# Attention with beacon keys and a max-out layer: values steps and second-layer tiles at other places of a written step list

## Chip, cores and metric

The kernel runs on one core of one Trainium2 chip. The metric is device time in microseconds from the start to the end of one execution; the figure of a kernel is the median over its runs. The profile is of one further execution, whose own time stands beside it.

## What is computed

```python
k_all = np.concatenate([beacon_k, k], axis=2)          # B, H, S, D = 8, 8, 576, 64; 16 beacons
v_all = np.concatenate([beacon_v, v], axis=2)
scores = scale * np.matmul(q, k_all.transpose(0, 1, 3, 2))
scores = np.where(causal, -1e9, scores)                # beacons are seen by every query
a = softmax(scores)
x = np.matmul(a, v_all)  -> (B * S, H * D) = (4608, 512)
h = np.maximum(np.maximum(x @ w1, x @ w2), x @ w3)     # 512 -> 768, three times
out = h @ w_out                                        # 768 -> 512, float32
```

## The kernel before

The whole program is one list of steps, `first_steps + loop_steps`, written out by hand. `emit_all` walks it from top to bottom and calls one helper for each step, so the order of the list is the order of the instructions on each of the engines; a step that issues on several engines takes its place in the order of each. No planner moves anything later. Engines wait for one another by semaphores only where a step reads what another has written, or where it reuses a tile.

The attention works on pairs of heads (32 pairs, four to a batch) and on quads, two pairs each (16 quads, two to a batch: quads 2b and 2b + 1 are of batch b). The steps that matter:

- `("scores", p, g, 0, place)` computes one of four groups of key tiles and queries for pair p: 2 or 4 matmuls (L513) into a PSUM tile, then one exponential on ScalarE (L522) into SBUF. `("mask", p, g, "pool")` zeroes the causal part there on POOL (L541). The groups of a pair come in the order 0, 2, 3, 1.
- `("values", quad, half, place)` is the softmax's sums and the product with v for one half of the queries of a quad, 120 matmuls for both halves (L582; 44 and 76). The first half needs groups 0, 2 and 3 of both pairs, the second needs all.
- `("invert",)` takes the reciprocal of the sums on ScalarE by a logarithm and an exponential (L603, L605); `("multiply", 3)` are three products on VectorE (L615) that write the quad's part of x; `("cross x", k, g, e, "pool")` copies it to the other half of the partitions on POOL (L680), which the first layer needs.
- `("unit", place)` is a piece of the first layer: 16 matmuls (L699) for 128 of the 768 outputs of one of the three weights and a block of tokens (two halves of 288), then a maximum (or, for the first weight, a copy) on VectorE into hT (L631, L629). There are 18 units to a block; the units of the block of batch b are dealt between the scores steps of batch b + 1, so that TensorE has work while ScalarE and POOL finish the scores.
- `("out", n, place)` is the second layer for n tiles of 128 tokens: 6 matmuls of 512 columns per tile (L725), a copy on VectorE (L733); `("store", 1)` sends the result by a DMA from the SP queue (L759).
- `("load", n)` issues the next input DMAs from the SP queue, behind a small memset on VectorE or POOL where an engine is named; `cast`, `cross`, `pair`, `keys` and `cast v` bring inputs into the form that scores and values need.

`place` is one of four PSUM tiles, 0 to 3. A step that takes a place waits until the step that had it before has been read out. Most places in the list are reused four uses later; some after two or three.

In a batch the list deals scores steps and units in turn. The values steps of the batch before come at two points: the even quad's ("first values steps") after unit 9 of the block, just behind the first two scores steps of the batch's third pair, and the odd quad's at the end of the block, behind unit 17. Quad 4 has its values step one unit earlier than the other even quads. An out of two tiles stands ahead of most first values steps and one of one to three tiles behind the last ones.

At the start, while the first inputs arrive, `("busy", n, cols)` issues n matmuls on a constant tile (L477).

Of the kernel before, what the change touches and what calls it, by code (L numbers as in the profile page):

```python
# [16 lines left out]
def kernel(  # L17
# [119 lines left out]
    busy = const.tile([128, 320], BF16, name="busy")  # L137
# [698 lines left out]
    def start_late():  # L836
# [62 lines left out]
        ("busy", 31, 174),  # L899
        ("identity",),  # L900
        ("busy", 12, 213),
# [230 lines left out]
        ("values", 4, 0, 2),  # L1132
        ("invert",),
        ("values", 4, 1, 3),
# [12 lines left out]
        ("mask", 10, 3, "pool"),  # L1147
        ("unit", 3),
        ("scores", 10, 1, 0, 0),
        ("mask", 10, 1, "pool"),  # L1150
        ("unit", 1),
        ("scores", 11, 0, 0, 2),
        ("mask", 11, 0, "pool"),
        ("unit", 3),
        ("load", 1, "pool"),
        ("scores", 11, 2, 0, 0),
        ("mask", 11, 2, "pool"),
        ("unit", 1),
# [3 lines left out]
        ("unit", 3),  # L1162
        ("scores", 11, 1, 0, 0),
        ("mask", 11, 1, "pool"),
        ("unit", 1),
# [3 lines left out]
        ("unit", 3),  # L1169
        ("values", 5, 0, 0),  # L1170
        ("invert",),
        ("values", 5, 1, 1),
# [8 lines left out]
        ("load", 1, None),  # L1181
        ("pair", 12, "act", "dve", 2),
        ("keys", 12, "act"),
        ("pair", 13, "act", "dve", 3),
        ("keys", 13, "act"),
        ("out", 2, 0),
        ("store", 1),
        ("out", 1, 1),
# [3 lines left out]
        ("unit", 3),  # L1192
        ("scores", 12, 2, 0, 0),
        ("mask", 12, 2, "pool"),
        ("unit", 1),
# [3 lines left out]
        ("load", 1, None),  # L1199
        ("scores", 12, 3, 0, 2),  # L1200
        ("mask", 12, 3, "pool"),
        ("unit", 3),
        ("scores", 12, 1, 0, 0),
        ("mask", 12, 1, "pool"),
        ("unit", 1),
        ("scores", 13, 0, 0, 2),
        ("mask", 13, 0, "pool"),
        ("unit", 3),
        ("cast v", 3, 0, "pool"),
        ("scores", 13, 2, 0, 0),  # L1210
        ("mask", 13, 2, "pool"),
        ("unit", 1),
# [4 lines left out]
        ("unit", 3),  # L1217
        ("cast v", 3, 1, "pool"),
        ("scores", 13, 1, 0, 0),
        ("mask", 13, 1, "pool"),  # L1220
        ("unit", 1),
        ("scores", 14, 0, 0, 2),
        ("mask", 14, 0, "pool"),
        ("unit", 3),
# [5 lines left out]
        ("scores", 14, 2, 0, 0),  # L1230
        ("mask", 14, 2, "pool"),
        ("unit", 1),
# [9 lines left out]
        ("cross x", 2, 0, 1, "pool"),  # L1242
        ("unit", 1),
        ("scores", 14, 3, 0, 2),
        ("mask", 14, 3, "pool"),
        ("unit", 3),
        ("load", 1, "pool"),
        ("scores", 14, 1, 0, 2),
        ("mask", 14, 1, "pool"),
        ("unit", 0),  # L1250
# [3 lines left out]
        ("scores", 15, 0, 0, 1),  # L1254
        ("mask", 15, 0, "pool"),
        ("unit", 3),
        ("keys", 16, "act"),
        ("scores", 15, 2, 0, 2),
        ("mask", 15, 2, "pool"),
        ("unit", 0),  # L1260
        ("load", 1, "pool"),
        ("scores", 15, 3, 0, 1),
        ("mask", 15, 3, "pool"),
        ("unit", 3),
        ("scores", 15, 1, 0, 2),
        ("mask", 15, 1, "pool"),
        ("unit", 0),
        ("unit", 1),
        ("values", 7, 0, 3),
        ("invert",),  # L1270
        ("values", 7, 1, 2),
# [8 lines left out]
        ("load", 1, None),  # L1280
        ("out", 2, 0),
        ("store", 1),
        ("scores", 16, 0, 0, 1),
        ("mask", 16, 0, "pool"),
        ("unit", 3),
        ("scores", 16, 2, 0, 2),
        ("mask", 16, 2, "pool"),
        ("unit", 1),
# [3 lines left out]
        ("load", 1, None),  # L1292
        ("keys", 17, "act"),
        ("scores", 16, 3, 0, 0),
        ("mask", 16, 3, "pool"),
        ("unit", 3),
        ("scores", 16, 1, 0, 2),
        ("mask", 16, 1, "pool"),
        ("unit", 1),
        ("scores", 17, 0, 0, 0),  # L1300
        ("mask", 17, 0, "pool"),
        ("unit", 3),
        ("cast v", 4, 0, "pool"),
        ("scores", 17, 2, 0, 2),
        ("mask", 17, 2, "pool"),
        ("unit", 1),
        ("load", 1, "pool"),
        ("keys", 18, "act"),
        ("scores", 17, 3, 0, 0),
        ("mask", 17, 3, "pool"),  # L1310
        ("unit", 3),
        ("cast v", 4, 1, "pool"),
        ("scores", 17, 1, 0, 2),
        ("mask", 17, 1, "pool"),
        ("unit", 1),
        ("scores", 18, 0, 0, 0),
        ("mask", 18, 0, "pool"),
        ("unit", 3),
# [5 lines left out]
        ("scores", 18, 2, 0, 2),  # L1324
        ("mask", 18, 2, "pool"),
        ("unit", 1),
        ("out", 2, 0),
        ("store", 1),
        ("values", 8, 0, 3),
        ("invert",),  # L1330
        ("values", 8, 1, 2),
# [5 lines left out]
        ("unit", 1),  # L1337
        ("scores", 18, 3, 0, 0),
        ("mask", 18, 3, "pool"),
        ("unit", 3),  # L1340
        ("load", 1, "pool"),
        ("scores", 18, 1, 0, 0),
        ("mask", 18, 1, "pool"),
        ("unit", 2),
# [3 lines left out]
        ("scores", 19, 0, 0, 1),  # L1348
        ("mask", 19, 0, "pool"),
        ("unit", 3),  # L1350
        ("keys", 20, "act"),
        ("scores", 19, 2, 0, 0),
        ("mask", 19, 2, "pool"),
        ("unit", 2),
        ("load", 1, "pool"),
        ("scores", 19, 3, 0, 1),
        ("mask", 19, 3, "pool"),
        ("unit", 3),
        ("scores", 19, 1, 0, 0),
        ("mask", 19, 1, "pool"),  # L1360
        ("unit", 2),
        ("unit", 1),
        ("values", 9, 0, 3),
        ("invert",),
        ("values", 9, 1, 0),
# [8 lines left out]
        ("load", 1, None),  # L1374
        ("out", 2, 2),
        ("store", 1),
        ("out", 1, 1),
        ("store", 1),
        ("scores", 20, 0, 0, 3),
        ("mask", 20, 0, "pool"),  # L1380
        ("unit", 0),
        ("scores", 20, 2, 0, 2),
# [5 lines left out]
        ("load", 1, None),  # L1388
        ("keys", 21, "act"),
        ("scores", 20, 3, 0, 3),  # L1390
        ("mask", 20, 3, "pool"),
        ("unit", 0),
        ("scores", 20, 1, 0, 2),
        ("mask", 20, 1, "pool"),
        ("unit", 1),
        ("scores", 21, 0, 0, 3),
        ("mask", 21, 0, "pool"),
        ("unit", 0),
        ("cast v", 5, 0, "pool"),
        ("scores", 21, 2, 0, 2),  # L1400
# [4 lines left out]
        ("scores", 21, 3, 0, 3),  # L1405
        ("mask", 21, 3, "pool"),
        ("unit", 0),
        ("cast v", 5, 1, "pool"),
        ("scores", 21, 1, 0, 2),
        ("mask", 21, 1, "pool"),  # L1410
        ("unit", 1),
        ("scores", 22, 0, 0, 3),
        ("mask", 22, 0, "pool"),
        ("unit", 0),
# [5 lines left out]
        ("scores", 22, 2, 0, 2),  # L1420
        ("mask", 22, 2, "pool"),
        ("unit", 1),
        ("out", 2, 3),
        ("store", 1),
        ("values", 10, 0, 0),
        ("invert",),
        ("values", 10, 1, 2),
# [4 lines left out]
        ("cross x", 4, 0, 1, "pool"),  # L1432
        ("unit", 1),
        ("scores", 22, 3, 0, 3),
# [5 lines left out]
        ("unit", 2),  # L1440
# [3 lines left out]
        ("scores", 23, 0, 0, 1),  # L1444
# [5 lines left out]
        ("unit", 2),  # L1450
        ("load", 1, "pool"),
        ("scores", 23, 3, 0, 1),
# [3 lines left out]
        ("mask", 23, 1, "pool"),  # L1456
        ("unit", 2),
        ("unit", 1),
        ("values", 11, 0, 0),
        ("invert",),  # L1460
        ("values", 11, 1, 3),
# [8 lines left out]
        ("load", 1, None),  # L1470
        ("out", 2, 2),
        ("store", 1),
        ("scores", 24, 0, 0, 1),
        ("mask", 24, 0, "pool"),
        ("unit", 0),
        ("scores", 24, 2, 0, 3),
        ("mask", 24, 2, "pool"),
        ("unit", 1),
# [3 lines left out]
        ("load", 1, None),  # L1482
# [4 lines left out]
        ("scores", 24, 1, 0, 3),  # L1487
        ("mask", 24, 1, "pool"),
        ("unit", 1),
# [4 lines left out]
        ("scores", 25, 2, 0, 3),  # L1494
        ("mask", 25, 2, "pool"),
        ("unit", 1),
# [6 lines left out]
        ("scores", 25, 1, 0, 3),  # L1503
        ("mask", 25, 1, "pool"),
        ("unit", 1),
# [8 lines left out]
        ("scores", 26, 2, 0, 3),  # L1514
        ("mask", 26, 2, "pool"),
        ("unit", 1),
        ("out", 2, 2),
        ("store", 1),
        ("values", 12, 0, 0),
# [6 lines left out]
        ("cross x", 5, 0, 1, "pool"),  # L1526
        ("unit", 1),
        ("scores", 26, 3, 0, 2),
        ("mask", 26, 3, "pool"),
        ("unit", 0),  # L1530
        ("load", 1, "pool"),
        ("scores", 26, 1, 0, 2),
        ("mask", 26, 1, "pool"),
        ("unit", 3),
# [5 lines left out]
        ("unit", 0),  # L1540
        ("keys", 28, "act"),
        ("scores", 27, 2, 0, 2),
        ("mask", 27, 2, "pool"),
        ("unit", 3),
        ("scores", 27, 3, 0, 1),
        ("mask", 27, 3, "pool"),
        ("unit", 0),
        ("scores", 27, 1, 0, 2),
        ("mask", 27, 1, "pool"),
        ("unit", 3),  # L1550
        ("unit", 1),
        ("values", 13, 0, 0),
        ("invert",),
        ("values", 13, 1, 2),
# [8 lines left out]
        ("out", 2, 3),  # L1563
# [3 lines left out]
        ("scores", 28, 0, 0, 0),  # L1567
        ("mask", 28, 0, "pool"),
        ("unit", 2),
        ("scores", 28, 2, 0, 3),  # L1570
# [6 lines left out]
        ("scores", 28, 3, 0, 0),  # L1577
        ("mask", 28, 3, "pool"),
        ("unit", 2),
        ("scores", 28, 1, 0, 3),  # L1580
        ("mask", 28, 1, "pool"),
        ("unit", 1),
        ("scores", 29, 0, 0, 0),
        ("mask", 29, 0, "pool"),
        ("unit", 2),
        ("cast v", 7, 0, "pool"),
        ("scores", 29, 2, 0, 3),
# [3 lines left out]
        ("scores", 29, 3, 0, 0),  # L1591
        ("mask", 29, 3, "pool"),
        ("unit", 2),
        ("cast v", 7, 1, "pool"),
        ("scores", 29, 1, 0, 3),
        ("mask", 29, 1, "pool"),
        ("unit", 1),
        ("scores", 30, 0, 0, 0),
        ("mask", 30, 0, "pool"),
        ("unit", 2),  # L1600
        ("keys", 31, "act"),
        ("scores", 30, 2, 0, 3),
        ("mask", 30, 2, "pool"),
        ("unit", 1),
        ("out", 2, 0),
        ("store", 1),
        ("values", 14, 0, 2),
# [6 lines left out]
        ("cross x", 6, 0, 1, "pool"),  # L1614
        ("unit", 1),
        ("scores", 30, 3, 0, 0),
        ("mask", 30, 3, "pool"),
        ("unit", 2),
        ("scores", 30, 1, 0, 0),
        ("mask", 30, 1, "pool"),  # L1620
        ("unit", 3),
        ("scores", 31, 0, 0, 1),
        ("mask", 31, 0, "pool"),
        ("unit", 2),
        ("scores", 31, 2, 0, 0),
        ("mask", 31, 2, "pool"),
        ("unit", 3),
        ("scores", 31, 3, 0, 1),
        ("mask", 31, 3, "pool"),
        ("unit", 2),  # L1630
        ("scores", 31, 1, 0, 0),
        ("mask", 31, 1, "pool"),
        ("unit", 3),
        ("unit", 1),
        ("values", 15, 0, 2),
        ("invert",),
        ("values", 15, 1, 0),
# [5 lines left out]
        ("out", 2, 3),  # L1643
        ("store", 1),
        ("out", 2, 1),
        ("store", 1),
        ("unit", 2, "act"),
        ("unit", 0, "act"),
        ("unit", 3, "act"),
        ("unit", 1, "act"),  # L1650
        ("unit", 2, "act"),
        ("unit", 0, "act"),
        ("unit", 3),
        ("unit", 1),
        ("unit", 2),
        ("unit", 0),
        ("unit", 3),
        ("unit", 1),
        ("unit", 2),
        ("unit", 0),  # L1660
        ("unit", 3),
        ("unit", 1),
        ("unit", 2),
        ("unit", 0),
        ("out", 2, 3),
        ("store", 1),
        ("out", 1, 1),
        ("store", 1),
        ("out", 1, 2),
        ("store", 1),  # L1670
        ("last", (0, 3), 0, 320, 512),
# [39 lines left out]
```

## Time and profile before

| | |
|---|---|
| median of 3 runs | 287.24 us (287.23 to 287.63) |
| the profiled execution | 289.68 us, span 287.9 us |
| TensorE busy | 277.3 us, 96% of the span |
| VectorE, ScalarE, POOL busy | 177.2, 155.0, 142.9 us |
| matmuls, weight loads | 5099 each |
| read from and written to HBM | 35.13 MB, 9.44 MB |

PE in the profile is TensorE's matmuls, PEld its weight loads, DVE VectorE, ACT ScalarE, SP the queue that issues most DMAs. Times in rows are microseconds from the start of the span. In a timeline a row gives start, length, engine, line, operation, tiles and how many were merged; in brackets stand the engine's idle time before it and what ended it. "issue" stands there where the engine waited for nothing that the profile shows.

### The profile page before, as it was taken

Reading aid. Unit: us, or ns where it says so; the run is one execution under the profiler, and the core shown is the slowest. Engines: PE = TensorE matmul, PEld = TensorE weight load, DVE = VectorE, ACT = ScalarE, POOL = GpSimd, SP = SyncE. Lnnn points to the kernel's source line nnn. Section 1 sums busy time; section 2 is a strip of 40 time slices with the busy share of each in tenths; the row PEclk is TensorE's granted clock in tenths of the full one; section 3 lists DMA queues with packets and bytes.
Section 4 is the critical chain, followed back from the end, with each engine's and each line's share of the span. In section 5 each row is a group of like instructions: output and inputs, shape, how many; then the busy total and the mean of one; then the engine's idle time right before and its main releaser. Section 6 shows DMA issues by size and latency. Waiting matters only on the chain.

```text
span 287.9 us, 11732 instructions
## 1 busy us (share of the span) xinstructions
PE 277.3 (96%) x5099; PEld 204.6 (71%) x5099; DVE 177.2 (62%) x331; ACT 155.0 (54%) x249; POOL 142.9 (50%) x296
## 2 busy tenths in 40 slices
PE   8997999999999999999999999989999999999995
PEld 7665777756777676868688676858678576867762
DVE  2456678885666765756576665746566665761654
ACT  2875577896463574737465473627455474624000
POOL 4463217897742485628843684628842682400000
PEclk9999999999999999999999999999999999999999
DMA  9999997999979299999999999997999551003004
GB/s 153 167 170 205 218 234 137 235 184 293 230 145 177 39 242 163 185 166 173 230 147 233 148 234 180 173 207 138 205 157 235 57 153 55 22 3 148 2 2 182
DMA packets 118307, 46.27 MB, mean 161 GB/s; under 512 B 107248, under 2 KB 112880, under 8 KB 118256
## 3 DMA queue, kind: packets, MB, share of 16 engines
q1 hardware_dynamic: 111888, 39.20, 75.4%
q0 software_dynamic: 5808, 6.00, 13.3%
q8 instruction: 40, 0.66, 1.0%
q10 hardware_dynamic: 560, 0.33, 0.4%
q14 instruction: 11, 0.09, 0.2%
HBM read 35.13 MB, written 9.44 MB: 155 GB/s over the span
## 4 chain that ended last, share of the span: by engine, by line
PE 85%; DMA 7%; issue 4%; POOL 1%; DVE 1%; POOLq 0%; DVEq 0%
PE t L699 44%; PE t L725 16%; PE t L582 10%; PE t L513 6%; DMA w_out_sb<-in_moe_w_out_dram 5%; DMA st<-in_v_dram 3%; PE pv L477 2%; PE pv L582 1%; PE sc L513 1%; PE t L397 1%; PE fps L637 1%; POOL at_sb L541 1%; PE sc L477 1%; POOL v_sb L315 1%; PE fps L582 0%
## 5 line engine op out<-in xcount | busy, mean ns | idle before, releaser
L699 PE MATMUL t<-xT,w_sb 64*128 64x288 bf16 (+1 forms) x1008 | 130.1, 285 | 0.7 <-issue 0.7
L699 PE MATMUL t<-xC,wC 64*128 64x288 bf16 (+1 forms) x1008 | 130.0, 284 | 0.0
L522 ACT ACTIVATE at_sb<-t 128x992 bf16<-128x992 f32 (+1 forms) x96 | 82.7, 864 | 40.7 <-PE t L513 35.6
L631 DVE TENSOR_TENSOR hT<-hT,t 128x576 bf16<-128x576 bf16 (+1 forms) x84 | 63.6, 763 | 31.1 <-PE t L699 31.1
L541 POOL TENSOR_SCALAR_AFFINE_SELECT at_sb<-at_sb 128x256 bf16<-128x256 bf16 (+2 forms) x143 | 54.3, 396 | 51.3 <-ACT at_sb L522 42.3
L699 PEld LDWEIGHTS <-w_sb 64*128 64x128 bf16 x1008 | 52.4, 94 | 12.5 <-issue 1.8
L699 PEld LDWEIGHTS <-wC 64*128 64x128 bf16 x1008 | 52.1, 94 | 11.4
L725 PE MATMUL t<-w_out_sb,hT 128*128 128x512 bf16 x210 | 47.7, 380 | 0.1
L680 POOL COPY xC<-xT 64x576 bf16<-64x576 bf16 (+1 forms) x26 | 18.2, 700 | 51.3 <-DVE xT L615 51.1
L629 DVE CAST hT<-t 128x576 bf16<-128x576 f32 (+1 forms) x36 | 27.7, 769 | 15.2 <-PE t L699 15.0
L725 PEld LDWEIGHTS <-hT 128*128 128x128 bf16 x210 | 19.4, 98 | 23.5 <-issue 1.4
L259 POOL CAST p<-st 96x768 bf16<-96x768 f32 x44 | 35.1, 825 | 0.3
L615 DVE TENSOR_TENSOR xT<-t,recip 128x288 bf16<-128x288 f32 (+2 forms) x78 | 23.1, 351 | 19.3 <-ACT recip L605 15.5
L733 DVE COPY y<-t 128x1024 f32<-128x1024 f32 (+1 forms) x20 | 21.8, 1092 | 20.1 <-PE t L725 19.7
L513 PE MATMUL t<-qT,kT 64*128 64x288 bf16 (+4 forms) x288 | 33.2, 279 | 0.0
L603 ACT ACTIVATE lnd<-t 128x288 f32<-128x288 f32 x26 | 10.7, 411 | 41.7 <-PE t L582 41.1
L582 PEld LDWEIGHTS <-v_sb 128*32 128x32 bf16 (+1 forms) x1408 | 24.9, 96 | 4.3 <-issue 3.1
L582 PE MATMUL t<-at_sb,v_sb 128*32 128x96 bf16 (+8 forms) x1144 | 24.3, 228 | 1.9 <-issue 1.8
L513 PEld LDWEIGHTS <-kT 64*128 64x128 bf16 x400 | 18.6, 94 | 10.4 <-issue 6.1
L522 ACT ACTIVATE at_sb<-sc 128x736 bf16<-128x736 f32 (+5 forms) x28 | 23.1, 861 | 3.7 <-PE sc L513 3.7
L315 POOL CAST v_sb<-st 128x1536 bf16<-128x1536 f32 (+2 forms) x21 | 18.4, 898 | 0.0
L582 PEld LDWEIGHTS <-ones 128*32 128x32 bf16 (+2 forms) x512 | 11.0, 95 | 7.3 <-issue 4.4
(125 smaller groups left out, 220.1 us busy)
## 6 DMA issues: line engine op xcount, KB each, us to landing
out_dram<-y SPq DMA_DIRECT2D x15, 512.0 KB, 5.6
st<-in_q_dram SPq DMA_DIRECT2D x24, 288.0 KB, 5.1
st<-in_k_dram SPq DMA_DIRECT2D x24, 288.0 KB, 5.7
st<-in_v_dram SPq DMA_DIRECT2D x24, 256.0 KB, 5.1
w_sb<-in_moe_w_dram POOLq DMA_DIRECT2D x6, 384.0 KB, 8.7
st<-in_v_dram SPq DMA_DIRECT2D x8, 224.0 KB, 3.9
st<-in_v_dram SPq DMA_DIRECT2D x8, 160.0 KB, 6.1
out_dram<-y SPq DMA_DIRECT2D x5, 256.0 KB, 3.2
```

What stands on the lines that cost most here:

```text
L259: cast(t16.rearrange("p r h d -> p h r d"), st[0:QP, i * NQ2 : (i + 1) * NQ2].rearrange("p (h r d) -> p h r d", h=2, r=QR),)
L315: cast(v_sb[0:n, t:t1].rearrange("p t h d -> p (t h d)"), st[0:n, (t - t_lo) * H * D : (t1 - t_lo) * H * D],)
L513: nc.tensor.matmul(ps[:, e, off : off + q1 - q0], kT[hs, 128 * t : 128 * t + 128], qT[hs, q0:q1], start=True, stop=True, tile_position=(64 ...
L522: nc.scalar.activation(out=both_heads(p, gi), in_=ps[:, :, 0 : g_width(p, gi)], func=AF.Exp, scale=scale)
L541: nc.gpsimd.affine_select(out=view, in_=view, compare_op=ALU.is_ge, fill=0.0, base=x0, pattern=[[0, 2], [1, hi - lo]], channel_multiplier=-1,)
L582: nc.tensor.matmul(ps[bank][32 * j : 32 * j + 32, lo + q0 - qa : lo + qb - qa], lhsT, at_view(PPQ * quad + j // 2, t, j % 2, q0, qb), star ...
L615: nc.vector.tensor_mul(xT[:, 2 * g + part - 1, c0 + ca : c0 + cb], ps[bank][:, lo : lo + cb - ca], recip[:, ca:cb],)
L629: (by_i or by_dve)(h, ps)
L631: nc.vector.tensor_max(h, h, ps)
L699: nc.tensor.matmul(ps[:, e], w[own(e), ct, cols], x, start=(ct == 0 and not over), stop=(ct == n_ct - 1 and over), tile_position=(64 * e, 0),)
L725: nc.tensor.matmul(ps[:, u], h_tile(tt + u, ft), w_out_sb[:, ft, :], start=(ft == 0), stop=(ft == n_ft - 1),)
L733: nc.vector.tensor_copy(y[:, 0:n], ps[:, 0:n])
```

## The change

Only the step list changes; no helper does. Each kind of step occurs as often as before.

- Opening: 31 matmuls of 174 columns become 27 of 200, and 12 of 213 become 16 of 160.
- First values steps: those of quads 6, 10, 12 and 14 (batches 3, 5, 6, 7), with their inverts, products and cross copies, come one scores step (group 2 of the third pair) and one unit sooner. That of quad 4 comes one scores step, one unit and two loads later. Quad 8's stays.
- Second-layer tiles: the out of two tiles ahead of quad 6's and quad 14's values step stays ahead of it; at quad 10 it goes behind; at quad 12 there is none any more, and two tiles stand between the halves of quad 11's values step; between those of quad 9's stands one tile that came behind it before.
- Places: renumbered throughout. At most steps the distance to the last use of the place is as before; near the moved steps it differs.
- `("load", 1, None)` becomes `("load", 1)`, which is the same call.

```diff
-        ("busy", 31, 174),
+        ("busy", 27, 200),
         ("identity",),
-        ("busy", 12, 213),
+        ("busy", 16, 160),
...
         ("scores", 10, 0, 0, 1),
         ("mask", 10, 0, "pool"),
         ("unit", 0),
-        ("values", 4, 0, 2),
-        ("invert",),
-        ("values", 4, 1, 3),
+        ("scores", 10, 2, 0, 2),
+        ("mask", 10, 2, "pool"),
+        ("unit", 3),
+        ("load", 1),
+        ("load", 1, "pool"),
+        ("values", 4, 0, 1),
+        ("invert",),
+        ("values", 4, 1, 0),
         ("multiply", 3),
         ("cross x", 1, 0, 0, "pool"),
         ("invert",),
         ("multiply", 3),
         ("cross x", 1, 0, 1, "pool"),
-        ("scores", 10, 2, 0, 1),
-        ("mask", 10, 2, "pool"),
-        ("unit", 0),
-        ("load", 1),
-        ("load", 1, "pool"),
-        ("unit", 2),
-        ("scores", 10, 3, 0, 1),
+        ("unit", 2),
+        ("scores", 10, 3, 0, 3),
...
-        ("scores", 14, 2, 0, 0),
+        ("out", 2, 3),
+        ("store", 1),
+        ("values", 6, 0, 0),
+        ("invert",),
+        ("values", 6, 1, 2),
+        ("multiply", 3),
+        ("cross x", 2, 0, 0, "pool"),
+        ("invert",),
+        ("multiply", 3),
+        ("cross x", 2, 0, 1, "pool"),
+        ("scores", 14, 2, 0, 1),
         ("mask", 14, 2, "pool"),
-        ("unit", 1),
-        ("out", 2, 2),
-        ("store", 1),
-        ("values", 6, 0, 3),
-        ("invert",),
-        ("values", 6, 1, 0),
...
-        ("values", 9, 0, 3),
-        ("invert",),
-        ("values", 9, 1, 0),
+        ("values", 9, 0, 2),
+        ("invert",),
+        ("out", 1, 1),
+        ("store", 1),
+        ("values", 9, 1, 3),
...
+        ("values", 10, 0, 3),
+        ("invert",),
+        ("values", 10, 1, 1),
+        ("multiply", 3),
+        ("cross x", 4, 0, 0, "pool"),
+        ("invert",),
+        ("multiply", 3),
+        ("cross x", 4, 0, 1, "pool"),
+        ("out", 2, 0),
+        ("store", 1),
         ("scores", 22, 2, 0, 2),
         ("mask", 22, 2, "pool"),
-        ("unit", 1),
-        ("out", 2, 3),
-        ("store", 1),
-        ("values", 10, 0, 0),
...
         ("values", 11, 0, 0),
         ("invert",),
-        ("values", 11, 1, 3),
+        ("out", 2, 3),
+        ("store", 1),
+        ("values", 11, 1, 1),
...
-        ("scores", 26, 2, 0, 3),
+        ("values", 12, 0, 1),
+        ("invert",),
+        ("values", 12, 1, 3),
+        ("multiply", 3),
+        ("cross x", 5, 0, 0, "pool"),
+        ("invert",),
+        ("multiply", 3),
+        ("cross x", 5, 0, 1, "pool"),
+        ("scores", 26, 2, 0, 2),
         ("mask", 26, 2, "pool"),
-        ("unit", 1),
-        ("out", 2, 2),
-        ("store", 1),
-        ("values", 12, 0, 0),
...
```

More of the change, by code (lines that the diff above doesn't have):

```diff
@@ L1242 @@
         ("cross x", 2, 0, 1, "pool"),
-        ("unit", 1),
[L1244 to L1249, printed above, removed]
-        ("unit", 0),
+        ("scores", 14, 2, 0, 1),
+        ("mask", 14, 2, "pool"),
+        ("unit", 3),
+        ("unit", 0),
+        ("scores", 14, 3, 0, 1),
+        ("mask", 14, 3, "pool"),
+        ("unit", 2),
+        ("load", 1, "pool"),
+        ("scores", 14, 1, 0, 3),
+        ("mask", 14, 1, "pool"),
+        ("unit", 1),
         ("cast", 17, "pool", "pool"),
@@ L1253 @@
         ("cross", 17, 1),
-        ("scores", 15, 0, 0, 1),
+        ("scores", 15, 0, 0, 0),
         ("mask", 15, 0, "pool"),
-        ("unit", 3),
+        ("unit", 2),
         ("keys", 16, "act"),
-        ("scores", 15, 2, 0, 2),
+        ("scores", 15, 2, 0, 3),
         ("mask", 15, 2, "pool"),
-        ("unit", 0),
[L1261 to L1269, printed above, removed]
+        ("unit", 1),
+        ("load", 1, "pool"),
+        ("scores", 15, 3, 0, 0),
+        ("mask", 15, 3, "pool"),
+        ("unit", 2),
+        ("scores", 15, 1, 0, 3),
+        ("mask", 15, 1, "pool"),
+        ("unit", 1),
+        ("unit", 0),
+        ("values", 7, 0, 2),
         ("invert",),
-        ("values", 7, 1, 2),
+        ("values", 7, 1, 3),
         ("multiply", 3),
@@ L1279 @@
         ("cross", 18, 1),
-        ("load", 1, None),
-        ("out", 2, 0),
+        ("load", 1),
+        ("out", 2, 1),
         ("store", 1),
-        ("scores", 16, 0, 0, 1),
+        ("scores", 16, 0, 0, 0),
         ("mask", 16, 0, "pool"),
-        ("unit", 3),
-        ("scores", 16, 2, 0, 2),
+        ("unit", 2),
+        ("scores", 16, 2, 0, 3),
         ("mask", 16, 2, "pool"),
-        ("unit", 1),
+        ("unit", 0),
         ("cast", 19, "pool", "pool"),
@@ L1323 @@
         ("keys", 19, "act"),
-        ("scores", 18, 2, 0, 2),
+        ("scores", 18, 2, 0, 3),
         ("mask", 18, 2, "pool"),
-        ("unit", 1),
-        ("out", 2, 0),
+        ("unit", 0),
+        ("out", 2, 1),
         ("store", 1),
-        ("values", 8, 0, 3),
+        ("values", 8, 0, 2),
         ("invert",),
-        ("values", 8, 1, 2),
+        ("values", 8, 1, 3),
         ("multiply", 3),
@@ L1336 @@
         ("cross x", 3, 0, 1, "pool"),
-        ("unit", 1),
-        ("scores", 18, 3, 0, 0),
+        ("unit", 0),
+        ("scores", 18, 3, 0, 1),
         ("mask", 18, 3, "pool"),
+        ("unit", 2),
+        ("load", 1, "pool"),
+        ("scores", 18, 1, 0, 1),
+        ("mask", 18, 1, "pool"),
         ("unit", 3),
[L1341 to L1344, printed above, removed]
         ("cast", 21, "pool", "pool"),
@@ L1432 @@
         ("cross x", 4, 0, 1, "pool"),
+        ("out", 2, 0),
+        ("store", 1),
+        ("scores", 22, 2, 0, 2),
+        ("mask", 22, 2, "pool"),
+        ("unit", 3),
         ("unit", 1),
-        ("scores", 22, 3, 0, 3),
+        ("scores", 22, 3, 0, 2),
         ("mask", 22, 3, "pool"),
@@ L1526 @@
         ("cross x", 5, 0, 1, "pool"),
+        ("scores", 26, 2, 0, 2),
+        ("mask", 26, 2, "pool"),
+        ("unit", 0),
         ("unit", 1),
@@ L1562 @@
         ("cross", 30, 1),
-        ("out", 2, 3),
+        ("out", 2, 2),
         ("store", 1),
@@ L1614 @@
         ("cross x", 6, 0, 1, "pool"),
+        ("scores", 30, 2, 0, 0),
+        ("mask", 30, 2, "pool"),
+        ("unit", 2),
         ("unit", 1),
```

285 lines of the change are left out of this document (137 added, 148 removed).

## The prediction

> **What bounds the kernel now.** I read the page first: busy time, slices, DMA queues.
>
> ```profile
> span 287.9 us, 11732 instructions
> PE 277.3 (96%) x5099; PEld 204.6 (71%) x5099; DVE 177.2 (62%) x331; ACT 155.0 (54%) x249; POOL 142.9 (50%) x296
> PEclk9999999999999999999999999999999999999999
> DMA  9999997999979299999999999997999551003004
> q1 hardware_dynamic: 111888, 39.20, 75.4%
> q8 instruction: 40, 0.66, 1.0%
> ```
>
> TensorE is busy 96% at full granted clock; no other engine passes 62%. From about 60 us to the end it is the bound, and only what makes it stand still or adds to its work can move the time. The DMA engines are full over most of the span. Queue q8 carries instructions: 40 packets for 5099 matmuls and 5099 weight loads, 10198 / 40 = 255 instructions a packet, or 127.5 matmuls with their loads.
>
> Next, what TensorE waited for, then the chain of waits around four places (start, length, what) and the matmuls in order of time.
>
> ```profile
> PE t L582 <- issue: 1.8, 2, 1.3
> PE t L699 <- issue: 0.7, 1, 0.7
> ```
>
> ```profile
> 76.70 1.78 PE t L582 x83
> 78.54 0.70 PE t L582 x37
> ...
> 113.15 2.29 PE t L582 x118
> ...
> 155.24 1.86 PE t L582 x86
> 157.90 3.99 PE t L725 x18
> ...
> 187.58 2.28 PE t L582 x116
> 189.86 1.26 issue
> 191.34 2.70 PE t L725 x12
> ```
>
> ```profile
> 213.47 0.30 PE L699 MATMUL t<-xC,wC 64*128 64x288 bf16 x2
> 214.49 0.30 PE L699 MATMUL t<-xT,w_sb 64*128 64x288 bf16 x2 [0.71 <-issue]
> ```
>
> An undisturbed values step (L582) takes 2.29 us, as that of quad 6 at 113.15. Quad 4 takes 79.25 - 76.70 = 2.55, quad 9 157.90 - 155.24 = 2.66, quad 11 191.34 - 187.58 = 3.76; and inside a unit at 213.47 the next pair comes 1.02 us later where 0.12 is the rule. The excess is 0.26 + 0.37 + 1.47 + 0.90 = 3.00 us. In the loop these are nearly all of TensorE's lost time, and the profile names no engine for them: "issue".
>
> What they share is found by counting matmuls from one restart to the next (columns: window, its length, then busy time and instructions of each engine, clock, DMA share, GB/s).
>
> ```profile
> 58.04:78.50 20.46, 20.18 (x383) 13.86 (x383) 13.48 (x20) 14.42 (x24) 17.60 (x27) 1.00 1.04 238
> 78.54:157.21 78.67, 78.56 (x1533) 59.71 (x1532) 50.75 (x84) 44.06 (x70) 42.77 (x92) 1.00 1.07 174
> 157.22:191.10 33.88, 32.65 (x638) 24.16 (x638) 20.83 (x36) 17.61 (x28) 19.50 (x40) 1.00 1.17 182
> 191.11:214.48 23.37, 22.65 (x382) 16.86 (x383) 14.00 (x23) 13.21 (x21) 14.68 (x30) 1.00 1.10 172
> ```
>
> 383, 1533, 638 and 382 are 3, 12, 5 and 3 times 127.3 to 127.8: whole numbers of q8 packets. So TensorE stops exactly where one packet's instructions are used up and the next has not come. I call 128 matmuls a packet's run. The runs that end in a stop, and two short ones that don't:
>
> ```profile
> 73.48:78.28 4.80, 4.80 (x132) 3.65 (x128) 2.93 (x4) 2.27 (x4) 4.14 (x9) 1.00 1.20 235
> 152.47:156.85 4.38, 4.38 (x133) 3.82 (x128) 2.58 (x4) 1.95 (x4) 0.83 (x4) 1.00 1.24 281
> 175.94:178.91 2.97, 2.97 (x128) 2.38 (x128) 1.99 (x4) 1.10 (x3) 0.00 (x0) 1.00 1.16 170
> 186.69:189.66 2.97, 2.97 (x132) 2.54 (x128) 1.71 (x3) 0.85 (x2) 0.14 (x1) 1.00 1.19 296
> 209.16:213.49 4.33, 4.33 (x144) 3.65 (x135) 3.16 (x9) 2.61 (x6) 1.28 (x2) 1.00 1.51 141
> 248.35:253.71 5.36, 5.36 (x128) 4.72 (x128) 3.77 (x5) 2.67 (x5) 1.89 (x5) 1.00 0.01 3
> ```
>
> From the start of such a run to the restart it took 78.54 - 73.48 = 5.06, 157.22 - 152.47 = 4.75, 191.11 - 186.69 = 4.42 and 214.49 - 209.16 = 5.33 us. I read that as the time a packet needs, from its request at the start of a run, beside full DMA queues (share 1.19 to 1.51). A values step has 120 matmuls in 2.29 us, so a run with a whole one in it is over before that. The run at 175.94 is as short and lost nothing, so the need can also be under 3 us; it is not constant.
>
> A rule to weigh: the Trainium skill, Runtime: NRT & Kernel Launch, section Instruction fetch mechanics, has instructions come in 16 KiB blocks of 256, the next fetched while the current one runs, and a crossing "mostly hidden". The block size agrees with 0.66 MB in 40 packets; the hiding does not hold in this trace, where four crossings cost 3.00 us. By the rule the sum below would keep only its costs.
>
> **The change part by part.**
>
> *Opening.* 31 x 174 = 5394 columns become 27 x 200 = 5400, and 12 x 213 = 2556 become 16 x 160 = 2560; 43 matmuls stay 43, so packet edges stay too.
>
> ```profile
> 7.42 0.16 PEld L359 LDWEIGHTS <-bk 16*128 16x128 bf16 x4 [0.22 <-ACT bk L860]
> ```
>
> What follows at 7.42 waits for ScalarE's cast, with 0.22 us idle. Zero; between -0.1 and +0.2 if the spare run ended later than the cast.
>
> *First values steps of quads 6, 10, 12, 14 a scores step and a unit sooner, quad 4 one later; outs moved.* TensorE's instructions stay the same in number; they are dealt differently over the runs. Prices, from the chain:
>
> ```profile
> 129.72 0.98 PE t L699 x16
> 130.70 0.20 PE t L513 x2
> 130.89 1.13 PE t L699 x16
> ...
> 173.62 2.70 PE t L725 x12
> ...
> 195.53 1.13 PE t L699 x16
> ```
>
> A unit is 16 matmuls in 0.98 (0.061 each), a scores step 2 or 4 in about 0.20, an out of two tiles 12 in 2.70, a values matmul 2.29 / 120 = 0.019. So what enters a run in place of values matmuls makes it longer:
> - Quad 4's run gains a unit and a scores step (18 matmuls, 0.98 + 0.20) for 18 values matmuls (0.34): 4.80 + 0.84 = 5.6; it needed 5.06.
> - Quad 9's gains the out of one tile between the halves (6, 1.3) for 6 values matmuls (0.11): 4.38 + 1.2 = 5.6; needed 4.75.
> - Quad 11's gains two tiles there (12, 2.70) for 0.23: 2.97 + 2.47 = 5.4; needed 4.42.
> - Quad 12 starts 18 matmuls sooner: its run from 209.16 gets a scores step and a unit (1.18) for 18 values matmuls: 4.33 + 0.84 = 5.2, against 5.33; the run ahead of it now holds 62 unit matmuls, three scores steps and 55 values matmuls, without the out: 62 x 0.061 + 3 x 0.20 + 55 x 0.019 = 5.4.
> - Quad 10's run (175.94) takes 12 out matmuls and a unit: 2.97 + 2.70 + 0.98 + 0.2 - 0.9 = 6.0.
>
> I take the four stops as gone but 0.1 each at quad 12's two runs: -3.00 + 0.2. Ends: none goes (0), and -3.00.
>
> *New wait.* At quads 7 and 11 the second unit behind the values step reuses the scores tile three uses back and takes 1.13 for 0.98 (130.89, 195.53): it waits for ScalarE's exponential. The new dealing does the same to the second unit behind quad 9: +0.15. All other reuses have a distance, or a pattern, that quads 4 to 8 show now; the reuses two back at quads 6, 10, 12, 14 go, which showed no wait.
>
> *One more change between out and the rest.* An out run of 12 takes 2.70, one of 18 takes 3.99: 6 matmuls 1.29, and 0.12 a run. Quad 9's 18 are split: +0.12.
>
> *Moves on other queues*, at nothing, under this cover:
>
> ```profile
> 80.08 0.93 ACT L522 ACTIVATE at_sb<-t 128x928 bf16<-128x928 f32 x1
> 80.20 0.89 DVE L615 TENSOR_TENSOR xT<-t,recip 128x288 bf16<-128x288 f32 x3 [0.85 <-ACT recip L605]
> 81.86 1.09 PE t L699 x16
> 204.26 0.33 POOL L541 TENSOR_SCALAR_AFFINE_SELECT at_sb<-at_sb 80x160 bf16<-80x160 bf16 x1
> 205.91 2.70 PE t L725 x12
> ```
>
> The sooner values step must find its masks. At quad 12 without the scores step and unit it starts about 204.6; its second half, 44 matmuls later, needs the mask that ends at 204.59: 0.7 us in hand. If POOL were later, that lateness is TensorE's. Behind the values step, the exponential of the next scores now queues on ScalarE behind both reciprocals, as at quad 4 today: it ends at 81.01, and VectorE's products at 81.09, 0.7 us or more ahead of the next users of their tiles there (scores, then the unit at 81.86); with units of 0.98 for 1.09 some 0.3 us stay in hand. At quads 9 and 11 the middle out's copy stands on VectorE ahead of the products; it is done about when the second half ends, 1 us before the second reciprocal. The cross copies on POOL come sooner, and the masks behind them are wanted five units later. On SP the stores move with their outs, by 2 to 4 us, and quad 4's two loads (with POOL's memset) go ahead of the cross copies; nothing on the chain behind 60 us waits for a load, so what they can do is shift DMA traffic against the instruction packets: between -1 and +1, taken as 0.
>
> **Sum** against the profiled execution's own 289.68 us (span 287.9, 1.8 around it): -3.00 + 0.20 + 0.15 + 0.12 = -2.53, so 287.15. The median of the runs shown, 287.24, is 2.44 under that execution, nearly the size of the stops, so they may be smaller without a profiler. The traffic that delays the packets is the kernel's own (q1 75.4%), which speaks for stops in every run. I take a packet's need as 0.3 us less there: stops of 0, 0.07, 1.17 and 0.60, 1.84 in all, none left after. 287.24 - 1.84 + 0.27 = 285.7.
>
> **The rivals.**
> 1. *The stops are the profiler's.* Then a usual run has none and only 0.15 + 0.12 stays: 287.5. For it: the 2.44 us. Against it: q1's share, and that the run at 248.35 without DMA traffic shows none. The skill's rule of hidden crossings, above, comes to the same 287.5.
> 2. *Slower: the packets come later where the stores and transposes now fall.* All the new runs are evened out at 5.2 to 6.0 us, five of them at 5.2 to 5.6. If the need there grows to 6.5 us, these lose about 5 x 1.1 = 5.5 in place of 1.84: 287.24 + 3.7 + 0.3 = 291.2; it decides from about 5.7 us on. Seen so far is 5.33 at most.
> 3. *The stops go in full in every run*: 287.24 - 2.73 = 284.5.
>
> **How the numbers follow.** Stops there in part or full and removed: 0.70 (rival 3 is 0.2 of that). Rival 1, or stops that only move: 0.17. Rival 2 or a late mask: 0.13. About 0.2% (0.57 us) is what a measurement of this kernel can tell from no change. The range goes from rival 3 to just past rival 1, 284.4 to 287.6; the likeliest case's own range is 284.5 to 286.6.
>
> **What would show it.** Right: values steps of quads 4, 9 and 11 and the unit behind quad 12 at 2.29 (halves with the out between) and 0.98, TensorE's "issue" waits behind 60 us under 0.7 us in sum, three units of 1.13 for two, a span near 285.4. Wrong: new "issue" stops at whole packets in the runs of quads 4, 9, 10, 11 or 12; a values step that waits for a mask; a first unit that waits for POOL's cross copy; or a profiled time that falls while the usual runs' does not.

## The result

The changed kernel takes 285.25 us (median of 11 runs, 284.71 to 286.71) against 287.61 us of before beside it (11 runs, 286.81 to 289.44): a ratio of 0.9921, 95% interval 0.9896 to 0.9947. Forecast were 285.7 us and faster.

The page of the profile after, in the order of the lines shown of before:

```profile
span 283.9 us, 11728 instructions
PE 276.3 (97%) x5099; PEld 201.9 (71%) x5099; DVE 176.9 (62%) x331; ACT 155.2 (55%) x249; POOL 141.8 (50%) x296
PEclk9999999999999999999999999999999999999999
DMA  8999999999978299999999999999997952004004
q1 hardware_dynamic: 111888, 39.20, 74.8%
q8 instruction: 40, 0.66, 1.0%
```

Work, clock and traffic are the same. Between the two profiles TensorE's busy time fell by 1.0 us and the span by 4.0; the rest is standing still that is gone. What TensorE waited for from 50 us to the end has one row left, and the chain of waits shows where it is and how the values steps now run:

```profile
PE t L582 <- issue: 0.6, 1, 0.6
```

```profile
56.94 2.01 PE t L582 x83
...
76.56 2.29 PE t L582 x110
...
153.55 0.79 PE t L582 x44
154.33 1.40 PE t L725 x6
155.73 1.61 PE t L582 x76
157.35 2.69 PE t L725 x12
...
161.54 1.13 PE t L699 x16
...
185.87 0.79 PE t L582 x44
186.65 2.69 PE t L725 x12
189.35 1.61 PE t L582 x76
...
204.36 2.29 PE t L582 x117
```

Quads 4 and 12 take 2.29 us, quads 9 and 11 take 0.79 + 1.61 = 2.40 with the out between, and no stop stands in any of them nor in the unit behind quad 12. A window over all of it says the same:

```profile
56.95:276.35 219.40, 219.40 (x4085) 1.00 0.86 154
```

TensorE is busy for all of 219.40 us, from the restart in quad 3's values step nearly to the end. That stop in quad 3, ahead of anything in the loop that the change moves, was there before as well (0.5 us, at 57.7).

From the first unit to the end it is 283.9 - 65.35 = 218.55 us now and was 287.9 - 66.77 = 221.1: 2.6 us less, where the sum had 2.53. The remaining 1.4 us of the spans' 4.0 lies ahead of the first unit, and is no part of the gain by the times: with the opening alone (below) the first unit starts at 65.31 us, 1.46 sooner than in the profile of before, and the time is the same. With before's own opening it starts at 65.01 us in the profile of the one-piece kernel below, so the late start is not the opening's.

### The profile page after: what moved, and what is told of

The parts are those of the page before. It is cut to its first block, busy times and chain, and to the rows that moved or that the text cites. A ratio compares the mean times of both kernels' runs of the same rounds, so it can differ in the third digit from the quotient of the medians.

```text
span 283.9 us, 11728 instructions
## 1 busy us (share of the span) xinstructions
PE 276.3 (97%) x5099; PEld 201.9 (71%) x5099; DVE 176.9 (62%) x331; ACT 155.2 (55%) x249; POOL 141.8 (50%) x296
## 4 chain that ended last, share of the span: by engine, by line
PE 90%; DMA 3%; ACT 2%; DVE 2%; POOL 1%; issue 1%; ACTq 0%; POOLq 0%
PE t L699 44%; PE t L725 16%; PE t L582 11%; PE t L513 6%; DMA w_sb<-in_moe_w_dram 3%; PE pv L477 2%; PE pv L637 2%; ACT at_sb L522 2%; PE sc L513 1%; PE sc L637 1%; PE t L397 1%; PE fps L637 1%; PE wide L582 1%; POOL p L259 1%; PE pv L582 0%
## 5 line engine op out<-in xcount | busy, mean ns | idle before, releaser
L541 POOL TENSOR_SCALAR_AFFINE_SELECT at_sb<-at_sb 128x256 bf16<-128x256 bf16 (+2 forms) x143 | 53.4, 389 | 54.0 <-ACT at_sb L522 43.8
L699 PEld LDWEIGHTS <-w_sb 64*128 64x128 bf16 x1008 | 51.5, 94 | 12.5 <-issue 1.1
L699 PEld LDWEIGHTS <-wC 64*128 64x128 bf16 x1008 | 51.2, 94 | 12.2
L582 PE MATMUL t<-at_sb,v_sb 128*32 128x96 bf16 (+8 forms) x1144 | 23.7, 228 | 0.6 <-issue 0.6
```

Of the source, the lines that this page charges most:

```text
L541: nc.gpsimd.affine_select(out=view, in_=view, compare_op=ALU.is_ge, fill=0.0, base=x0, pattern=[[0, 2], [1, hi - lo]], channel_multiplier=-1,)
L582: nc.tensor.matmul(ps[bank][32 * j : 32 * j + 32, lo + q0 - qa : lo + qb - qa], lhsT, at_view(PPQ * quad + j // 2, t, j % 2, q0, qb), star ...
L699: nc.tensor.matmul(ps[:, e], w[own(e), ct, cols], x, start=(ct == 0 and not over), stop=(ct == n_ct - 1 and over), tile_position=(64 * e, 0),)
```

## The experiments

Two theories stand against each other at the start. *Packet theory*: TensorE stops where one instruction packet is used up and the next has not come, and the change deals the steps so that every packet's run is long enough. *Data theory*: the new order gives masks, exponentials or tiles more time, and the stops' places have nothing to do with how many instructions went before. A third possibility is that the opening's edit carries part of the gain.

### The opening alone, and the loop alone

The first kernel is before with the two lines of the opening; the second is the change without them.

```diff
-        ("busy", 31, 174),
+        ("busy", 27, 200),
         ("identity",),
-        ("busy", 12, 213),
+        ("busy", 16, 160),
```

> Before, with only the opening of the change (27 x 200 and 16 x 160 columns). Packet theory: 43 matmuls stay 43, so no packet edge moves and the four stops stay: within 0.3 us of before. Opening theory: 1.0 to 1.4 us faster.

> The change with the opening of before (31 x 174 and 12 x 213 columns). Packet theory: the gain comes from the loop, where the profiles show 230.8 us behind the first values step of quad 3 (57.07 to 287.9) against 228.2 (55.71 to 283.9): 2.0 to 2.6 us faster than before, about 285.2. Opening theory: the first 57 us were 1.36 us shorter in the profile after, so without the new opening 1.0 to 1.4 us of the gain go: about 286.4.

Measured: the opening alone 287.49 us against 287.52, ratio 0.9997 (0.9974 to 1.0019): nothing. The loop alone 286.12 us, ratio 0.9953 (0.9926 to 0.9981): 1.4 us faster, with no stop behind quad 3 in its profile. By the number that misses the packet theory's 2.0 to 2.6 us and lies nearer to the opening theory's 286.4. But the opening by itself gives nothing, and the change itself, run again further down, has 0.9950, the same as the loop alone. So the gain is put down to the loop, and its size lies between the 1.4 us here and the 2.4 us of the first comparison. The kernel with the opening alone has before's loop, so its profile is a second one of that order:

```profile
PE t L582 <- issue: 1.3, 2, 1.0
PE t L699 <- issue: 0.3, 1, 0.3
```

They are at quads 3 (0.3) and 11 (1.0) and behind quad 12 (0.3). Counted by the length of the step, as in the prediction, quad 11 loses 1.2 us here (1.47 in the first profile), quad 9 0.15 (0.37) and quad 4 nothing (0.26). So the stops that come stand at the same places, and their sizes vary from one execution to the next. The span of this profile was 285.2 against 287.9: of the 2.7 us between the two, 1.46 lie ahead of the first unit and 1.2 in the loop, which is the same in both.

### The change with 36 more matmuls ahead of it

```diff
-        ("busy", 27, 200),
+        ("busy", 60, 90),
         ("identity",),
-        ("busy", 16, 160),
+        ("busy", 19, 135),
```

> The change, with 36 more matmuls in the opening and the same columns (60 x 90 and 19 x 135 = 5400 and 2565), so that every packet edge falls 36 matmuls earlier in the loop. Packet theory: with the prices of the prediction, runs of 4.2, 2.7, 2.9, 3.7 and 2.8 us appear near quads 4, 5, 10, 12 and 13, so new stops without an engine's name in about these values steps, 4 to 8 us in all: 289 to 293 us. Data theory (the new order only gives masks, exponentials and tiles more time): the loop has the same order, so no stops and 285.3 us, within 0.5 of the change.

Measured: 291.91 us, ratio 1.0148 (1.0103 to 1.0193). The loop's order is untouched, and the same order is now 4.4 us slower than before. The data theory falls. TensorE's waits behind 50 us:

```profile
PE t L582 <- issue: 2.6, 1, 2.6
PE pv L637 <- issue: 0.9, 1, 0.9
PE t L699 <- issue: 0.6, 1, 0.6
PE t L725 <- DVE xT L615: 0.6, 1, 0.6
PE t L725 <- issue: 0.2, 1, 0.2
```

Only a part of the expectation held. Stops came at 54.5 and 59.6 us (ahead of and in quad 3's values step), at 153.7 us (in a unit) and at 224.9 us (behind quad 13); at quads 4, 5, 10 and 12, where the runs shrank to 2.7 to 4.2 us, none did. A short run is a risk, not a stop. The fourth row, which the profile puts down to VectorE's product, is the stop behind quad 13; it stands at a packet edge (counted in the next section), so I count it with the others. The fifth is at 63.1 us, 12 matmuls behind an edge, while the clock was low.

That the time fell into the expected 289 to 293 us is in part luck. Of the stops, 3.5 us lie ahead of the loop, and the loop has 1.2 us of them where 4 to 8 were expected. Still, from the first unit (70.31) to the end (290.4) it takes 220.1 us in place of the change's 218.55, with the same order of steps. The stop of 2.6 us cost more than itself (columns: window, length, TensorE's busy time and matmuls, granted clock, DMA share, GB/s):

```profile
59.40:62.20 2.80, 0.24 (x22) 0.94 0.82 151
62.20:65.40 3.20, 2.98 (x17) 0.52 0.97 229
65.40:70.00 4.60, 4.60 (x41) 1.00 0.82 232
```

The granted clock was 0.50 from 61.84 to 65.25 us, which makes the 0.52 of the second window. It is not the whole of the loss: two of the four runs had a mean clock of 1.000 and took 290.12 and 291.64 us.

### Before with 12 more matmuls ahead of it

```diff
-        ("busy", 31, 174),
+        ("busy", 43, 126),
```

> Before, with 12 more matmuls in the opening and about the same columns (43 x 126 = 5418 for 31 x 174 = 5394), every packet edge 12 matmuls earlier. Packet theory: the run that ends in quad 4 goes from 4.6 to 6 us and loses its stop, quad 9's from 4.2 to 4.7, quad 11's only from 2.9 to 3.4 and quad 12's shrinks from 4.3 to 3.9: stops of about 0, 0.1, 0.9 and 1.4 for 0.26, 0.37, 1.47 and 0.90, so 0.3 to 1 us faster, and the stops stand at other matmuls. Data theory: the four stops stay at their matmuls, within 0.3 us of before.

Measured: 288.27 us, ratio 1.0038 (1.0013 to 1.0063). The sign was missed: slower, not faster. The places were right (the chain of waits of this kernel; before's rows are in the prediction):

```profile
74.70 1.53 PE t L582 x71
76.23 0.42 issue
...
185.66 2.16 PE t L582 x104
187.82 0.67 issue
188.49 0.34 PE t L582 x12
```

Quad 4's stop came behind 71 matmuls, in before behind 83: 12 earlier, as the edge. Weight loads give the count more exactly, since a few matmul records are missing from most of the traces and no load is. In quad 11, 14 loads are left when the stop comes, in before 2: 12 again. The same count from the start of the execution to the middle of a stop shows what all the stops share (window, its length, then the loads' busy time and number, clock, DMA share, GB/s):

```profile
0.00:190.50 190.50, 136.98 (x3543) 1.00 1.09 188
0.00:214.10 214.10, 153.84 (x3926) 1.00 1.09 186
```

```profile
0.00:188.20 188.20, 136.41 (x3543) 1.00 1.11 190
0.00:211.20 211.20, 152.80 (x3926) 1.00 1.10 188
```

```profile
0.00:225.20 225.20, 159.80 (x4181) 0.99 1.05 185
```

The first two rows are before's stops in quad 11 and behind quad 12, the next two those of before with 12 more matmuls, and the last is the stop behind quad 13 in the change with 36 more. The numbers 3543 and 3926 are the same in both kernels although other matmuls stand there, and the distances are 3 x 127.7 and 2 x 127.5. Over all profiles of this document, 29 such stops of more than 0.15 us come behind 50 us (the 0.2 us at 63.1 above is not one of them). Their counts are whole numbers of packets apart, and in each the last packet of q8 had landed 1.25 to 1.82 us before TensorE went on. That is the packet theory seen directly.

The sizes were missed. By the length of the step quad 4 loses 0.7 us (0.26 in before, 0 expected), quad 11 0.9 (as expected) and quad 9 nothing; behind quad 12 there is a wait of 1.0 (1.4 expected). The expectation said that quad 4's run would grow to 6 us; 12 unit matmuls for 12 values matmuls make it 4.6 + 12 x (0.068 - 0.019) = 5.2. Ahead of the loop a stop of 0.5 came in a pair step at 60.5 us, while quad 3 lost its own. Why the median is 0.8 us above before's is not shown: the profiled execution, 287.47 us, is the shortest of the ten. The sizes of stops in a given run cannot be worked out from the run's length alone.

### One piece of the change: the out between quad 11's halves

```diff
         ("values", 11, 0, 0),
         ("invert",),
-        ("values", 11, 1, 3),
+        ("out", 2, 3),
+        ("store", 1),
+        ("values", 11, 1, 2),
...
-        ("out", 2, 2),
-        ("store", 1),
         ("values", 12, 0, 0),
```

> Before, with one edit of the change: the out of two tiles ahead of quad 12's first half goes between the halves of quad 11's values step, and the places behind it are renumbered. Packet theory: quad 11's run grows from 2.97 to 5.4 us and loses its stop (1.47 and 1.16 us in the two profiles with the old order); quad 12's run and the others keep theirs: 0.8 to 1.5 us faster, no stop in quad 11. Rival (the gain came from all of the new order at once, from tiles and masks with more time): next to nothing, within 0.3 us.

Measured: 286.77 us, ratio 0.9964 (0.9934 to 0.9994), 0.8 us by the medians and 0.2 to 1.9 by the interval. Its chain has quad 11 without a stop, and the waits of the same profile still have those at quads 3 and 9 and behind quad 12:

```profile
185.64 0.79 PE t L582 x44
...
189.12 1.61 PE t L582 x76
```

```profile
PE t L699 <- issue: 0.6, 1, 0.6
PE t L582 <- issue: 0.4, 2, 0.2
```

So the piece takes away its own quad's stop and leaves the others (quad 4's, which comes and goes between the profiles of before's order, is absent here). By the medians it is a third of the gain in the first comparison and half of that in the second, with intervals that leave this wide.

### Is it the DMA traffic that makes the packets late?

v is read as rows of 512 values in place of 8 of 64, and late q and k as the early ones; the first kernel is before, the second the change with 36 more matmuls.

```diff
-            if p < P_X:
+            if True:
...
-            out=dst[lo : lo + n], in_=v[b, :, t0 : t0 + n, :].rearrange("h p d -> p h d")
+            out=dst[lo : lo + n],
+            in_=v[b].rearrange("h s d -> (h s d)").rearrange("(p h d) -> p h d", h=H, d=D)[t0 : t0 + n],
```

> Before, with v and the late q and k read in longer rows (v as rows of 512 values in place of 8 of 64, q and k of all pairs as those of the first 14): the same bytes in far fewer DMA packets, and the tokens in another order, so the output is of other rows than the reference's. If the time of an instruction packet is set by the kernel's own DMA traffic, the stops in the loop fall to under 1 us in sum (3.0 in the profile of before), 1.5 to 3 us faster. If it is a fixed need of an instruction packet, quads 9, 11 and 12 stop as before and the time is within 0.5 us.

> The change with 36 more matmuls in the opening (291.9 us, stops of 0.9, 2.6, 0.6 and 0.6 us and a slow clock behind the second) and with the longer rows of v, q and k, which change the output's rows. If traffic sets the need: the stops at quads 3, 9 and 13 fall to under 1 us in sum, 284 to 287 us. If not: above 289 us with the same stops.

Measured: 287.03 us, ratio 0.9994 (0.9959 to 1.003), and 292.23 us, ratio 1.0171 (1.0113 to 1.023). Neither is faster by its median. In these kernels the lines stand 2 lower, so L584 is the values step, L727 the out and L639 a matmul of the first layer ahead of the loop. Before with long rows, its waits behind 50 us and its steps of quads 9 and 11:

```profile
PE t L727 <- issue: 1.1, 1, 1.1
```

```profile
154.33 2.29 PE t L584 x117
...
186.29 2.34 PE t L584 x120
```

The one stop is at 62.1 us, ahead of the first unit. In the loop none is left: quads 4 and 9 take 2.29 us and quad 11 2.34. From the first unit (66.11) to the end (284.4) it takes 218.3 us, where the profile of before had 221.1 and the change has 218.55. So this profile meets what was expected if traffic sets the need, and the times do not: five of the ten runs took 285.69 to 286.25 us, the profiled one among them, and five 287.80 to 288.85. Without traces of the second five it stays open what they lost and where.

The change with 36 more and long rows, its waits behind 50 us:

```profile
PE t L584 <- issue: 3.1, 1, 3.1
PE t L727 <- issue: 2.8, 2, 1.5
PE pv L639 <- issue: 0.6, 1, 0.6
```

Ahead of the loop stand 0.6 and 3.1 us. In the loop stand 1.3 behind quad 10 and 1.5 behind quad 13, against 0.6 and 0.6 with short rows; the stop at 153.7 us is gone, and that behind quad 10 is new. The DMA queue of this kernel over 100 to 240 us, and that of the change in the same window:

```profile
q1 hardware_dynamic: 34208, 24.52, 79.7%
```

```profile
q1 hardware_dynamic: 78176, 24.72, 105.1%
```

Less than half the packets and three quarters of the queue's time for nearly the same bytes, and still bigger stops in this kernel, while before's loop lost its stops. So short rows are not needed for a stop, and the two profiles do not settle what they add. The DMA records of the traces say a little more. Between quads 4 and 13, from the start of a packet's run to the start of the transfer of the next packet on q8, 1.1 to 1.6 us pass on average in the eleven profiles with short rows, and 0.8 and 0.7 in the two with long rows. But each of these two has a wait of 2.7 to 3.0 us as well. Traffic thus shows in the average wait; what makes the long ones is open, and no run changed the count of transfers under way or their bytes.

### The edges moved a little: 8 less, 6 more, 10 more

```diff
-        ("busy", 27, 200),
+        ("busy", 19, 284),
```

with 33 of 164 and 37 of 146 in the other two. The change itself ran again beside the latter.

> The change with 8 matmuls less in the opening and the same columns (19 x 284 = 5396 for 27 x 200), every packet edge 8 matmuls later: can another place of the edges beat the change? Packet theory: by the prices all runs of the loop stay at 4.8 us or more, so still no stop behind quad 3; the edges of the first 57 us move too, and there the stops (0.6 us in quad 3) may go either way: within 0.7 us of the change, 284.6 to 286.

> The change with 6 matmuls more in the opening and about the same columns (33 x 164 = 5412 for 27 x 200), every packet edge 6 matmuls earlier. 8 fewer made the stop in quad 3 1.6 us long for 0.6 us. Packet theory: in the loop all runs stay at 4.8 us or more and no stop comes; if the stop in quad 3 shrinks the other way, 0.2 to 0.6 us faster than the change, else equal to it. Rival (edges don't matter in this range): equal to the change within 0.2 us.

> The change with 10 matmuls more in the opening (37 x 146 = 5402), every edge 10 earlier. Packet theory: the run near quad 12 falls to 4.7 us and may stop for up to 0.6 us; quad 3 as with 6 more, or the stop goes over into the pair step behind it, as with 12 more in before (0.5 us): between 0.5 faster and 0.6 slower than the change.

> The change itself on the same chip and beside the same runs of before as the two with more matmuls: 0.990 to 0.995 of before by the packet theory, no stop behind quad 3 in its profile, and in quad 3 about 0.6 us.

| matmuls against the change | median, us | ratio to before (interval) | stops behind 50 us in the profile |
|---|---|---|---|
| 8 less | 286.20 | 0.9956 (0.9928 to 0.9984) | 1.6, quad 3 |
| none (again) | 285.85 | 0.9950 (0.9930 to 0.9971) | 0.6, quad 3; 0.4, behind quad 12 |
| 6 more | 285.44 | 0.9935 (0.9915 to 0.9955) | none |
| 10 more | 285.39 | 0.9924 (0.9894 to 0.9953) | 0.6, a pair step; 0.5, scores behind quad 12 |

Waits behind 50 us with 8 less, and with 10 more:

```profile
PE t L582 <- issue: 1.6, 1, 1.6
```

```profile
PE t L397 <- issue: 0.6, 1, 0.6
PE t L513 <- issue: 0.5, 1, 0.5
```

All four stay below before. In the loop the only stops are 0.4 and 0.5 us behind quad 12, at the run that the prediction had as the shortest against its need; the others stand ahead of the loop and change with each shift. Two expectations were missed by a little: 286.20 us with 8 less lies above the 286 given, and the change run again has a stop behind quad 12 where none was expected. With 6 more the profile has no wait of TensorE behind 50 us (span 283.5 us), but its time is not clear of the change's: the intervals overlap. No version was found that beats the change by more than these can tell.

## Why the prediction was right

- *What bounds the kernel, and that the four stops are packet edges.* Shown: with 12 more matmuls ahead two stops move by 12, to the same counts of weight loads as before, and all stops of all profiles stand whole packets apart. That the edges alone can cost time is shown by 36 more ahead of an unchanged loop (1.0148), though most of that loss lies ahead of the loop.
- *The new runs.* No stop in any of the five quads in the profile after; in the second profile of the change 0.4 us stood behind quad 12, the run that the prediction had as the shortest against its need (5.2 against 5.33) and priced at 0.1.
- *The added costs.* The third unit of 1.13 is there (161.54): +0.15. Quad 9 with its outs was priced at 2.29 + 3.99 + 0.12 = 6.40 and takes 0.79 + 1.40 + 1.61 + 2.69 = 6.49. Quad 11's split was priced at nothing and costs 0.1: its two halves take 2.40 for 2.29. From the first unit to the end the two profiles differ by 2.6 us, where the sum had 2.53.
- *What was held to be covered.* The mask of quad 12 ended at 203.88 + 0.33 = 204.21, and the values step began at 204.36; its second half, which needs this mask, follows 0.8 us later, so 0.9 us were in hand where the prediction had 0.7. At quad 11 the copy of the middle out ends at 189.38 + 1.23 = 190.61, about when the second half does (190.96), as I had it. The products of the first half start only at 190.53, those of the second at 191.99; TensorE shows no wait for either:

```profile
203.88 0.33 POOL L541 TENSOR_SCALAR_AFFINE_SELECT at_sb<-at_sb 80x160 bf16<-80x160 bf16 x1
```

```profile
189.38 1.23 DVE L733 COPY y<-t 128x1024 f32<-128x1024 f32 x1 [2.72 <-PE t L725]
190.53 0.88 DVE L615 TENSOR_TENSOR xT<-t,recip 128x288 bf16<-128x288 f32 x3
191.99 0.89 DVE L615 TENSOR_TENSOR xT<-t,recip 128x288 bf16<-128x288 f32 x3 [0.58 <-issue]
```

- *The opening at nothing.* Shown: 0.9997.
- *Where it was off.* The step from the profiled execution to the median. I took the 2.44 us between them as a sign that stops are smaller without a profiler, cut a packet's need by 0.3 us, and so came from 2.53 to a gain of 1.57. The reason was wrong: the second profile of before's loop was taken by the same profiler and is 2.7 us shorter, of which 1.46 us lie ahead of the first unit and have nothing to do with these stops. What the 2.44 us was is scatter; before's runs go from 286.81 to 289.44 in one comparison. The stops that the cut left (0, 0.07, 1.17 and 0.60) are near those of the second profile (0, 0.15, 1.2 and a wait of 0.3), and that is luck. Whether 1.57 or 2.53 is the better size stays open: the medians differ by 2.4 in the first comparison, with 1.5 to 3.0 by the interval, and by 1.5 in the second (287.39 against 285.85). Rival 3, the full gain at 284.5, is 0.75 us from the 285.25 measured, the forecast 0.45.
- *The rivals.* That the stops are the profiler's falls with the timed gain. That packets come later at the new places did not happen at this placing of the edges; 36 matmuls more show that it can, and cost 4.4 us against before.
- *A reading that stays open.* I held the kernel's full DMA queues for what makes a packet late. Long rows shortened the average wait for a packet's start and took the stops out of before's loop in one profile, but left long stops in the other kernel and no gain in the medians. Nor is a packet always asked for at the start of a run, as I read it: some transfers began up to 1.2 us ahead of that (last section).

## What to carry to other kernels

When the busiest engine's waits say "issue" and name nobody, count its instructions between them: whole multiples of one number point to instruction supply, and then the dense bursts of short matmuls are what to spread, so that each packet holds slower ones too. Such a schedule is tuned to a count: any edit ahead of it that adds or drops a few dozen instructions can undo it, so compare variants at the same count, or measure at several. Take more than one profile before the gap between a profiled execution and the median is put down to one term of the sum.

## What the hardware showed unexpectedly

- At a stop of 2.6 us, and again at one of 3.1 us (the change with 36 more matmuls, short and long rows), TensorE's granted clock fell to 0.50 for 3.41 us, so one long stop cost more than its length. In the profiles whose longest stop was 1.6 us or less no such drop shows.
- Runs as short as 2.7 to 2.9 us passed without a stop in some places, and runs of about 5 us stopped in others. The DMA records of before show where the difference lies. Between quads 4 and 13 a packet's transfer takes 0.9 to 1.4 us, but it starts anywhere from 1.2 us ahead of the run's start to 2.7 us behind it; the packet that the run at 175.94 us waits for at its end had started at 175.62, and that short run lost nothing. What sets this start is not settled here.
